# Issuing the first x load of a streaming kernel as two transfers, rows 0 to 15 and rows 16 to 127

## Chip, cores and metric

The kernel runs on one core of a Trainium2 chip. The metric is the device time in microseconds (us); lower is better. Runs of one kernel agree within about half a per cent here, with an occasional run 1% off. "Span" is the time from the first to the last instruction of the one profiled execution; the timed run is about 1.8 us longer (152.39 us for a span of 150.6 us).

## The reference

```python
B, S, D = 512, 32, 640          # bfloat16
def reference(x, fx, alpha):    # x, fx: [B, S, D]; alpha: [1]
    return x + alpha * fx
```

## The kernel before

The tensors are viewed as 128 rows of 81,920 bf16 elements, one row for each SBUF partition, and are worked through in five chunks of 16,384 columns. A chunk of x or fx is 128 rows of 32 KB, 4 MiB. All large transfers are issued by SyncE, in a fixed order. VectorE does one fused multiply-add for each chunk, in place in the x buffer, and the x buffer is then stored.

```python
xv = x.flatten_outer_dims().rearrange("(p n) d -> p (n d)", p=P)   # fxv, ov alike
xs = ctx.enter_context(tc.tile_pool(name="xs", bufs=4))
fs = ctx.enter_context(tc.tile_pool(name="fs", bufs=2))
ctx.enter_context(tc.manual_schedule())
# ... cut: alpha is put on all lanes by one tiny load, a matmul and a copy ...

def load_x(k):
    xt[k] = xs.tile([P, CHUNK], x.dtype, tag="x", name="x_t")
    nc.sync.dma_start(out=xt[k][:], in_=xv[:, bass.ts(k, CHUNK)])

def load_f(k):
    ft[k] = fs.tile([P, CHUNK], fx.dtype, tag="f", name="f_t")
    nc.sync.dma_start(out=ft[k][:], in_=fxv[:, bass.ts(k, CHUNK)])
# ... cut: compute(k, parts) is one scalar_tensor_tensor per part; store(k, j, parts) one DMA ...

load_x(0); load_f(0); load_x(1); load_f(1); load_x(2)
compute(0); load_f(2); store(0); load_x(3)
compute(1); load_f(3); store(1); load_x(4)
compute(2); load_f(4); store(2)
compute(3); store(3)
compute(4, 2); store(4, 0, 2); store(4, 1, 2)
```

## Time and profile before

| quantity | before |
|---|---|
| time, median of 4 runs | 152.93 us (152.51 to 153.17) |
| span of the profiled run | 150.6 us |
| bytes moved by DMA | 62.92 MB, 418 GB/s over the span |
| VectorE busy | 86.9 us, 58% |
| first compute starts | 22.84 us |

These lines are from the page of the kernel before: engine shares, the DMA rows of the 40 time slices (tenths of full, then GB/s), the DMA queues, the chain of waits that ended last, and the loads with their size and the time from issue to landing (the median, where a line holds several).

```profile
span 150.6 us, 85 instructions
PE 0.2 (0%) x1; PEld 0.1 (0%) x1; DVE 86.9 (58%) x8; POOL 0.2 (0%) x4
...
DMA  6999999999999999799999999999999999999994
GB/s 200 444 453 435 418 418 418 418 444 453 444 453 435 418 418 418 339 444 470 418 418 418 418 418 435 435 435 453 426 435 444 418 418 435 435 435 405 426 444 205
...
q1 hardware_dynamic: 2304, 62.92, 98.0%
...
DMA 56%; DVE 29%; DVEq 6%; issue 0%; SPq 0%
...
x_t<-in_x_dram SPq DMA_DIRECT2D x5, 4096.0 KB, 34.8
f_t<-in_fx_dram SPq DMA_DIRECT2D x5, 4096.0 KB, 32.1
```

The DMA engines are full from the second slice to the last but one. The chain of waits names VectorE for 29%, but while it computes, the queue behind it stays full, so I would not expect a faster VectorE to end the kernel sooner. The bound is the DMA stream.

The next lines are windows of the same run; the last two columns are the mean busy share of the 16 DMA engines and the GB/s they moved. A transfer's bytes are counted where their packet starts, so the GB/s of a short window swing around the true rate.

```profile
0.00:8.00 8.00, 0.16 (x1) 0.10 (x1) 0.32 (x2) 0.20 (x4) 1.00 0.85 328
8.00:16.00 8.00, 0.00 (x0) 0.00 (x0) 0.00 (x0) 0.00 (x0) 1.00 1.01 434
16.00:24.00 8.00, 0.00 (x0) 0.00 (x0) 1.16 (x1) 0.00 (x0) 1.00 0.97 418
```

And these are its computes in the timeline: start and duration in us, and in brackets how long VectorE had been idle and what ended the idle time.

```profile
22.84 17.28 DVE L69 SCALAR_TENSOR_TENSOR x_t<-f_t,a_f,x_t 128x16384 bf16<-128x16384 bf16 x1 [20.57 <-DMA f_t<-in_fx_dram]
42.25 17.28 DVE L69 SCALAR_TENSOR_TENSOR x_t<-f_t,a_f,x_t 128x16384 bf16<-128x16384 bf16 x1 [2.12 <-DMA f_t<-in_fx_dram]
62.24 17.28 DVE L69 SCALAR_TENSOR_TENSOR x_t<-f_t,a_f,x_t 128x16384 bf16<-128x16384 bf16 x1 [2.71 <-DMA f_t<-in_fx_dram]
91.71 17.29 DVE L69 SCALAR_TENSOR_TENSOR x_t<-f_t,a_f,x_t 128x16384 bf16<-128x16384 bf16 x1 [12.19 <-DMA f_t<-in_fx_dram]
120.91 17.42 DVE L69 SCALAR_TENSOR_TENSOR x_t<-f_t,a_f,x_t 128x8192 bf16<-128x8192 bf16 x2 [11.91 <-DMA f_t<-in_fx_dram]
```

The trace also holds a record of each packet (`prof` doesn't print them; they were read from the trace file). A packet here is one row of one transfer, 32 KB, moved by one of the 16 DMA engines; at 20, 30, 80 and 100 us of the span 16 of them are under way. The first row of each engine takes 1.6 to 2.4 us, and nearly all others take about 1.213 us, which is 27 GB/s for an engine. Each engine moves the equivalent of 120 such rows: 120 x 1.213 = 145.6 us of the 150.6 us span.

### The profile page before, as it was taken

To read this page: it belongs to the slowest core of one execution; us is meant where nothing else is said; L and a number is where in the kernel's file an instruction comes from. 1 tells how busy PE (TensorE), PEld (TensorE's weight loads), DVE (VectorE), ACT (ScalarE), POOL (GpSimd) and SP (SyncE) were. 2 spreads that over 40 slices of the span, in tenths; PEclk is the share of its full clock that TensorE was granted. 3 is DMA by queue.
4 is the path that set the end of the run, shared out by engine and by line. 5 is a ranking of instruction groups with operands and counts; after the bars stand their busy time and mean duration, and the time that the engine had idled before them with its cause. 6 is when DMAs were issued, how large, how long until landed. Compare 5 with 4: busy or idle time off the path is not lost.

```text
span 150.6 us, 85 instructions
## 1 busy us (share of the span) xinstructions
PE 0.2 (0%) x1; PEld 0.1 (0%) x1; DVE 86.9 (58%) x8; POOL 0.2 (0%) x4
## 2 busy tenths in 40 slices
PE   0000000000000000000000000000000000000000
PEld 0000000000000000000000000000000000000000
DVE  0000009999679998499991006999900089997000
POOL 0000000000000000000000000000000000000000
DMA  6999999999999999799999999999999999999994
GB/s 200 444 453 435 418 418 418 418 444 453 444 453 435 418 418 418 339 444 470 418 418 418 418 418 435 435 435 453 426 435 444 418 418 435 435 435 405 426 444 205
DMA packets 2306, 62.92 MB, mean 418 GB/s; under 512 B 258, under 2 KB 258, under 8 KB 258
## 3 DMA queue, kind: packets, MB, share of 16 engines
q1 hardware_dynamic: 2304, 62.92, 98.0%
q10 hardware_dynamic: 2, 0.00, 0.0%
HBM read 41.94 MB, written 20.97 MB: 418 GB/s over the span
## 4 chain that ended last, share of the span: by engine, by line
DMA 56%; DVE 29%; DVEq 6%; issue 0%; SPq 0%
DMA f_t<-in_fx_dram 56%; DVE x_t L69 29%; DVEq L131 6%; SPq L59 0%; DVEq L69 0%
## 5 line engine op out<-in xcount | busy, mean ns | idle before, releaser
L69 DVE SCALAR_TENSOR_TENSOR x_t<-f_t,a_f,x_t 128x16384 bf16<-128x16384 bf16 (+1 forms) x6 | 86.6, 14439 | 49.5 <-DMA f_t<-in_fx_dram 49.5
L26 DVE COPY a_f<-a_ps 128x1 f32<-128x1 f32 x1 | 0.2, 159 | 1.1 <-PE a_ps L24 1.1
L22 DVE MEMSET ones<- 1x128 bf16 x1 | 0.2, 165 | 0.8 <-PEq L120 0.8
L24 PE MATMUL a_ps<-a,ones 1*128 1x1 bf16 x1 | 0.2, 159 | 1.9 <-DMA a<-in_alpha_dram 1.9
L120 POOL MEMSET const-bfloat16-1.0<- 128x1 bf16 x1 | 0.1, 102 | 0.0
L120 POOL MEMSET const-uint8-127<- 128x1 uint8 x1 | 0.1, 102 | 0.0
L24 PEld LDWEIGHTS <-ones 1*128 1x128 bf16 x1 | 0.1, 100 | 1.0 <-DVE ones L22 1.0
L120 POOL MEMSET const-float32-0.0<- 128x1 f32 x1 | 0.1, 99 | 0.2 <-issue 0.2
L120 POOL MEMSET const-float32-1.0<- 128x1 f32 x1 | 0.1, 99 | 0.0
## 6 DMA issues: line engine op xcount, KB each, us to landing
x_t<-in_x_dram SPq DMA_DIRECT2D x5, 4096.0 KB, 34.8
f_t<-in_fx_dram SPq DMA_DIRECT2D x5, 4096.0 KB, 32.1
out_dram<-x_t SPq DMA_DIRECT2D x4, 4096.0 KB, 36.5
out_dram<-x_t SPq DMA_DIRECT2D x2, 2048.0 KB, 15.2
a<-in_alpha_dram ACTq DMA_DIRECT2D x1, 0.0 KB
```

What stands on the lines that cost most here:

```text
L22: nc.vector.memset(ones[:], 1.0)
L24: nc.tensor.matmul(a_ps[:], ones[:], a_1[:], start=True, stop=True)
L26: nc.vector.tensor_copy(out=a_f[:], in_=a_ps[:])
L69: nc.vector.scalar_tensor_tensor(out=xt[k][:, s], in0=ft[k][:, s], scalar=a_f[:], in1=xt[k][:, s], op0=ALU.mult, op1=ALU.add,)
L120: nc = _bacc.Bacc("TRN2", target_bir_lowering=False, num_devices=1)
L131: with _tile.TileContext(nc) as tc:
```

## The change

The likely intent is to get the DMA engines going sooner: a small transfer of 16 rows is put in front, and the other 112 rows follow at once. The bytes, the computes and the order of everything else stay as they are.

```diff
     def load_x(k):
         xt[k] = xs.tile([P, CHUNK], x.dtype, tag="x", name="x_t")
-        nc.sync.dma_start(out=xt[k][:], in_=xv[:, bass.ts(k, CHUNK)])
+        for a, b in [(0, 16), (16, P)] if k == 0 else [(0, P)]:
+            nc.sync.dma_start(out=xt[k][a:b, :], in_=xv[a:b, bass.ts(k, CHUNK)])
```

## The prediction

> **What bounds the kernel now.** DMA. The page's queue part gives 62.92 MB in a 150.6 us span and 98.0% of 16 engines' time; only the first and last slices are not full. DVE is busy 58%; on the chain of waits it appears (29%) only because it stands between transfers, while the queue stays full behind it. In the trace's packet records each of the 16 DMA engines moves 120 rows' worth of 32 KB at a median 1.213 us: 120 x 1.213 = 145.6 us. The rest is about 1.6 us before the first packet, 1.5 us of slower packets where stores begin, and 1.3 us of completion. Whatever slows all DMA engines anywhere is paid in full.
>
> **What the change does.** It removes no work and adds no bytes. It adds one issue on SyncE (0.38 to 0.57 us each in the timeline), hidden behind the first packets (1.6 to 2.4 us), and a second completion to wait for (tens of ns; DVE waits for f_t, not x_t). Possible gain: 16 rows may reach all engines sooner; before's first packets start over 0.42 us, so at most about 0.3 us.
>
> **The cost I expect** is how the rows meet SBUF. [...] Before's trace agrees only in that 128 rows run at 16 x 27 GB/s; it has no narrow load. Estimates with the trace's 1.213 us:
> - Rows 0 to 15 are one row per engine[...].
> - Rows 16 to 127 are 7 rows per engine. [...]
> - Together +3 to +8 us. [...]
>
> **On the critical path: all of it.** The queue never drains, so the delay moves f_t's first landing (22.7 us), every compute and the last store alike. Nothing later gives it back.
>
> **Prediction: 158.5 us**, 80% range 153.0 to 163.5. Faster by over 2%: 0.02; within 2%: 0.25; slower by over 2%: 0.73.
>
> **What would show each step.**
> - [...]
> - Collisions in the 112-row load: packets of about 2.4 us among the next 112, and engines out of step afterwards; then 1.213 us again.
> - Shift: the first DVE compute starts at 26 to 31 us instead of 22.8; later gaps are unchanged; the span grows by the same amount; DVE busy stays 86.9 us.
>
> **What would make it wrong.** If [...]engines have enough in flight to hide it, only tenths of a us remain: 152.9 to 153.5 us. [...]

The forecast's sum stands: +3 to +8 us, with 158.5 us (152.93 + 5.57) as the central value.

## The result and the profile after

| quantity | before | after |
|---|---|---|
| time, median of 4 runs | 152.93 us | 162.26 us (162.13 to 162.70) |
| span of the profiled run | 150.6 us | 160.4 us |
| bytes | 62.92 MB | 62.92 MB |
| VectorE busy | 86.9 us | 86.9 us |
| first compute starts | 22.84 us | 32.31 us |

The ratio is 1.0619, with a 95% interval of 1.0583 to 1.0654. A ratio is the mean time of one kernel's fast runs over that of the other's of the same rounds, so it is not quite the ratio of the medians. The changed kernel is slower by 6%.

The same lines of the page after the change:

```profile
span 160.4 us, 88 instructions
PE 0.2 (0%) x1; PEld 0.1 (0%) x1; DVE 86.9 (54%) x8; POOL 0.2 (0%) x4
...
DMA  9799999999999999999999999999999999999991
GB/s 131 139 261 286 253 351 441 449 417 425 449 433 400 457 441 400 441 466 400 433 449 425 425 449 417 408 449 441 417 417 474 392 417 466 417 425 425 400 445 53
...
q1 hardware_dynamic: 2320, 62.92, 97.1%
...
DMA 59%; DVE 27%; DVEq 5%; SPq 0%; issue 0%
...
f_t<-in_fx_dram SPq DMA_DIRECT2D x5, 4096.0 KB, 31.3
x_t<-in_x_dram SPq DMA_DIRECT2D x4, 4096.0 KB, 39.8
...
x_t<-in_x_dram SPq DMA_DIRECT2D x1, 3584.0 KB, 21.3
x_t<-in_x_dram SPq DMA_DIRECT2D x1, 512.0 KB, 7.2
```

The busy row of the DMA engines is as full as before, from the first slice on. Only the GB/s row below it shows the loss: five slices of about 4 us at 131 to 286 GB/s instead of some 430. The engines are busy, but with rows that take longer. The windows and the computes say the same:

```profile
0.00:8.00 8.00, 0.16 (x1) 0.10 (x1) 0.32 (x2) 0.20 (x4) 1.00 0.85 135
8.00:16.00 8.00, 0.00 (x0) 0.00 (x0) 0.00 (x0) 0.00 (x0) 1.00 1.01 270
16.00:24.00 8.00, 0.00 (x0) 0.00 (x0) 0.00 (x0) 0.00 (x0) 1.00 0.98 307
24.00:32.00 8.00, 0.00 (x0) 0.00 (x0) 0.00 (x0) 0.00 (x0) 1.00 1.03 442
```

```profile
32.31 17.29 DVE L70 SCALAR_TENSOR_TENSOR x_t<-f_t,a_f,x_t 128x16384 bf16<-128x16384 bf16 x1 [30.02 <-DMA f_t<-in_fx_dram]
51.71 17.28 DVE L70 SCALAR_TENSOR_TENSOR x_t<-f_t,a_f,x_t 128x16384 bf16<-128x16384 bf16 x1 [2.12 <-DMA f_t<-in_fx_dram]
71.13 17.29 DVE L70 SCALAR_TENSOR_TENSOR x_t<-f_t,a_f,x_t 128x16384 bf16<-128x16384 bf16 x1 [2.13 <-DMA f_t<-in_fx_dram]
100.43 17.28 DVE L70 SCALAR_TENSOR_TENSOR x_t<-f_t,a_f,x_t 128x16384 bf16<-128x16384 bf16 x1 [12.02 <-DMA f_t<-in_fx_dram]
130.55 17.41 DVE L70 SCALAR_TENSOR_TENSOR x_t<-f_t,a_f,x_t 128x8192 bf16<-128x8192 bf16 x2 [12.83 <-DMA f_t<-in_fx_dram]
```

The five computes start 9.47, 9.46, 8.89, 8.72 and 9.64 us later than before, and the span is 9.8 us longer. Nearly the whole loss thus arises before the first compute and stays. The packet records show where. Here are the first rows of each engine, sixteen records at a time in the order of their starts; before, the means are 1.93 us and then 1.21 to 1.23 us:

```
after: n-th row of the 16 engines, us: shortest / mean / longest
row 0 (the 16-row transfer)  2.40 / 3.73 / 4.31
row 1 (112-row transfer)     2.57 / 2.91 / 3.67
row 2                        2.18 / 2.25 / 2.29
row 3                        1.45 / 1.68 / 2.08
row 4                        1.68 / 1.85 / 2.20
row 5                        1.72 / 2.00 / 2.41
row 6                        2.02 / 2.15 / 2.22
row 7                        1.98 / 2.07 / 2.29
row 8 (fx load)              1.50 / 1.71 / 2.00
row 9                        1.21 / 1.23 / 1.27
```

### The profile page after: what moved, and what is told of

Read it like the earlier page. It is cut to its first block, busy times and chain, and to the rows that moved or that the text cites. A ratio compares the mean times of both kernels' runs of the same rounds, so it can differ in the third digit from the quotient of the medians.

```text
span 160.4 us, 88 instructions
## 1 busy us (share of the span) xinstructions
PE 0.2 (0%) x1; PEld 0.1 (0%) x1; DVE 86.9 (54%) x8; POOL 0.2 (0%) x4
## 2 busy tenths in 40 slices
DMA packets 2322, 62.92 MB, mean 392 GB/s; under 512 B 274, under 2 KB 274, under 8 KB 274
## 3 DMA queue, kind: packets, MB, share of 16 engines
q1 hardware_dynamic: 2320, 62.92, 97.1%
## 4 chain that ended last, share of the span: by engine, by line
DMA 59%; DVE 27%; DVEq 5%; SPq 0%; issue 0%
DMA f_t<-in_fx_dram 59%; DVE x_t L70 27%; DVEq L132 5%; SPq L60 0%; DVEq L70 0%
```

## The experiments

The main theory is that of the prediction: how long a row takes depends on which SBUF partitions the rows of its transfer hit. The texts call it the port theory. That engines meet and share something at some partitions, and the word "port" for it, are my guess: the traces show the time of each row, but no ports, and not which engine wrote which partition. "Consecutive" and "round robin" are two guesses of how the rows of a transfer are dealt to the engines, and no trace shows which it is. The rivals are:

- A: two transfers cost more than one, however they are cut (issue, completion, a small first transfer).
- B: a transfer of fewer than 128 rows is slow by its shape.
- C: it is the rows of HBM that matter.
- D, added later ("foreign port" in the texts): each engine is fast only to the partitions that it has in a 128-row load.

Runs called "extra" are the kernel before with one or more loads added at the very front of the queue, into a buffer that is loaded again with the proper data later; all of them give correct results. (Their diffs below show the added load alone.) In their traces, the start of the first compute, less 22.84 us, is what the load cost. The record does not name the chip of the trace of before, and the others come from three chips, but the median row takes 1.213 to 1.215 us in all of them. Each of these starts is read from one trace. Timed ratios are to runs of before on the same chip.

### The same split by columns

```diff
+        for a, b in [(0, 2048), (2048, CHUNK)] if k == 0 else [(0, CHUNK)]:
+            nc.sync.dma_start(out=xt[k][:, a:b], in_=xv[:, k * CHUNK + a : k * CHUNK + b])
```

> The first x load is again two transfers of one eighth and seven eighths of its bytes, but cut by columns (2048 and 14336 of 16384), so that both have 128 rows. Port theory (the loss comes from which SBUF partitions the rows of a transfer hit): nothing is lost, 152.5 to 153.8 us, first compute at 22.4 to 23.2 us. Rival A (two transfers, one more issue, one more completion or a small first transfer cost the time, however they are cut): about 162 us as after the change, first compute at about 32 us.

Measured: 153.00 us against 152.84 us for before, ratio 1.0026 (0.9966 to 1.0085): no difference. The loads in the page of this run, and its first compute:

```profile
x_t<-in_x_dram SPq DMA_DIRECT2D x1, 3584.0 KB, 11.5
x_t<-in_x_dram SPq DMA_DIRECT2D x1, 512.0 KB, 3.3
```

```profile
22.56 17.29 DVE L70 SCALAR_TENSOR_TENSOR x_t<-f_t,a_f,x_t 128x16384 bf16<-128x16384 bf16 x1 [20.27 <-DMA f_t<-in_fx_dram]
```

The same two sizes, the same number of issues and completions, and no loss: rival A falls. The first 512 KB land 3.3 us after issue when cut by columns and 7.2 us when they are rows 0 to 15, a difference of 3.9 us. The first compute starts 0.28 us sooner than before, about the gain that the change may have been after. That is one trace against one; the time does not show a gain, and by the last compute the two kernels are level (120.94 and 120.91 us).

### Sixty-four rows, two places

```diff
+    nc.sync.dma_start(out=xt[3][0:64, :], in_=xv[0:64, bass.ts(3, CHUNK)])    # one run
+    nc.sync.dma_start(out=xt[3][32:96, :], in_=xv[0:64, bass.ts(3, CHUNK)])   # the other
```

> The kernel before with one extra load put first on the queue: 64 rows of 32 KB into partitions 0 to 63 of a buffer that is not needed until later. Its bytes alone are 4 rows per DMA engine, 4 x 1.213 = 4.85 us. Port theory with consecutive rows per engine: [...]162.4 to 163 us. [...] Rival B (a transfer of fewer than 128 rows is slow by its shape alone, whatever its partitions): the same time as the next run. No effect of either: 157.8 us.

> The same extra load of the same 64 rows of HBM, but into partitions 32 to 95. Port theory with 4 consecutive rows per engine: [...]157.5 to 158.3 us, 4 to 5.2 us less than the run at partition 0. [...] Rival B (shape) and rival C (the rows in HBM): the same time as the run at partition 0.

Measured: 162.97 us at partition 0 (ratio 1.0668, interval 1.0611 to 1.0725) and 158.15 us at partition 32 (1.0365, 1.0312 to 1.0417), with 152.84 us for before. The extra load's line in the page, first at partition 0, then at partition 32:

```profile
x_t<-in_x_dram SPq DMA_DIRECT2D x1, 2048.0 KB, 13.5
```

```profile
x_t<-in_x_dram SPq DMA_DIRECT2D x1, 2048.0 KB, 7.7
```

Shape, bytes and HBM rows are the same; only the SBUF partitions differ, and 4.8 us come and go with them. Rivals B and C fall. In the packet records the rows at partition 0 take 2.57 us after the first, and those at partition 32 take 1.21 to 1.26 us on average.

### Eight transfers of sixteen rows

```diff
+        for a, b in [(16 * i, 16 * i + 16) for i in range(8)] if k == 0 else [(0, P)]:
+            nc.sync.dma_start(out=xt[k][a:b, :], in_=xv[a:b, bass.ts(k, CHUNK)])
```

> The first x load cut into eight transfers of 16 rows. Each gives one row to each engine[...]. Port theory, engines that cannot run ahead: [...]about 177 to 182 us. Port theory, engines that run ahead by most of a row: about 163 to 167 us. If the 112 rows of the changed kernel are dealt round robin, they are the same as seven such transfers, and this run equals the changed kernel, 162 us; if they are consecutive, it is slower than that. Rival A (a cost for each transfer added): 153 + 7 x 9.3 = 218 us. No dependence on rows: 153 to 156 us.

Measured: 177.76 us, ratio 1.1620 (1.1572 to 1.1668). The GB/s row of its page:

```profile
GB/s 119 119 119 119 119 119 119 119 238 402 431 469 372 469 439 394 476 402 431 469 387 454 431 402 476 402 424 439 402 469 424 417 431 417 439 446 409 413 431 227
```

The time is in the range expected for engines that cannot run ahead (177 to 182 us), and much less than the 218 us of a cost for each transfer. It is also far slower than the changed kernel (162.26 us), so the 112 rows there do not cost what seven transfers of 16 rows do. Rows 1 to 7 of each engine take 4.46 us on average in the packet records, 3.7 times the 1.213 us of a row in a 128-row load; the timeline agrees, with SyncE's next four issues 4.45 to 4.47 us apart (8.14, 12.59, 17.05 and 21.52 us).

### The two halves of the change by themselves

```diff
+    nc.sync.dma_start(out=xt[3][0:16, :], in_=xv[0:16, bass.ts(3, CHUNK)])          # 16 rows
+    nc.sync.dma_start(out=xt[3][0:128:8, :], in_=xv[0:16, bass.ts(3, CHUNK)])       # 16 rows, spread
+    nc.sync.dma_start(out=xt[3][0:128, 0:2048],                                     # same bytes, 128 rows
+                      in_=xv[0:128, 3 * CHUNK : 3 * CHUNK + 2048])
+    nc.sync.dma_start(out=xt[3][16:128, :], in_=xv[16:128, bass.ts(3, CHUNK)])      # 112 rows
```

(One of these lines in each run.)

> The kernel before with an extra load of 16 rows of 32 KB into partitions 0 to 15 of the idle buffer, first on the queue: the first half of the change measured by itself. Its bytes are one row per engine, 1.213 us. Port theory: [...]157.3 to 158.2 us. No port effect for so short a load: 154.1 us.

> The same 16 rows of HBM and the same 16 descriptors, but into every eighth partition (0, 8, ... 120)[...]. Port theory: [...]154.9 to 155.8 us, about 2.4 us less than with partitions 0 to 15. Rival B (a load of 16 rows is slow because of its shape): the same as with partitions 0 to 15.

> The same 512 KB as 128 rows of 4 KB, into all partitions. Port theory: only the bytes, 1.2 us, so 153.8 to 154.5 us. It shows what 512 KB more cost[...].

> The kernel before with an extra load of 112 rows into partitions 16 to 127 of the idle buffer: the second half of the change by itself. Its bytes are 7 rows per engine, 8.5 us, so 161.4 us without collisions. Port theory with consecutive rows and fair sharing, no running ahead: [...]166.2 us. If the halves add up, [...]the run takes about 167 us. [...]

| extra load | time (before: 153.34 us) | ratio, interval | landing after issue | first compute later by | its bytes alone | loss (later by, less bytes) |
|---|---|---|---|---|---|---|
| 16 rows, partitions 0 to 15 | 156.15 us | 1.0190 (1.0142 to 1.0237) | 6.9 us | 4.20 us | 1.21 us | 2.99 us |
| 16 rows, every 8th partition | 155.01 us | 1.0125 (1.0078 to 1.0172) | 5.4 us | 2.61 us | 1.21 us | 1.40 us |
| 128 rows of 4 KB | 153.92 us | 1.0053 (1.0010 to 1.0095) | 3.9 us | 1.32 us | 1.21 us | 0.11 us |
| 112 rows, partitions 16 to 127 | 167.74 us | 1.0941 (1.0883 to 1.0999) | 17.4 us | 14.81 us | 8.49 us | 6.32 us |

The order is as expected: the same 512 KB cost least on all 128 partitions (first compute later by 1.32 us), more on every 8th partition (2.61 us) and most on partitions 0 to 15 (4.20 us). From one to the next the times differ by about 1.1 us, and the intervals of neighbours overlap; the order stands more clearly in the landings and first computes. The size for 16 rows was missed: 156.15 us is below the 157.3 to 158.2 us expected, and 1.14 us above the run with every 8th partition where about 2.4 us were expected. Why the short load costs less than expected is not shown. The 112 rows cost more than the 166.2 us of the estimate with fair sharing, and about the 167 us expected if the halves add up. The first computes of the runs with 16 rows on partitions 0 to 15 and with 112 rows, from which the losses are taken:

```profile
27.04 17.29 DVE L70 SCALAR_TENSOR_TENSOR x_t<-f_t,a_f,x_t 128x16384 bf16<-128x16384 bf16 x1 [24.74 <-DMA f_t<-in_fx_dram]
37.65 17.28 DVE L70 SCALAR_TENSOR_TENSOR x_t<-f_t,a_f,x_t 128x16384 bf16<-128x16384 bf16 x1 [35.36 <-DMA f_t<-in_fx_dram]
```

At the first compute the halves do add up: 2.99 + 6.32 = 9.31 us, against 9.47 us in the changed kernel.

In the packet records of the 112-row run the seven rows take 2.05 us on average, and after the first row no engine has a row below 1.65 us. That was unexpected: by my estimate, which no trace shows, only some of the 16 engines would meet at any step. The last four runs ask why all of them were slow.

### Sixty-four rows, two more places

```diff
+    nc.sync.dma_start(out=xt[3][36:100, :], in_=xv[0:64, bass.ts(3, CHUNK)])   # one run
+    nc.sync.dma_start(out=xt[3][48:112, :], in_=xv[0:64, bass.ts(3, CHUNK)])   # the other
```

"Independent" stands for engines that slow down without slowing the others, "coupled" for all being slowed together. How many engines would meet at each place was my estimate.

> The extra load of 64 rows again, now into partitions 36 to 99. [...] It asks why the 112 rows slowed all 16 engines alike (rows of 1.65 to 2.3 us each)[...]. Theory independent: most rows of the extra load take 1.21 us, 2 of 16 take 2.4 or more. Theory coupled[...]: all 16 engines' rows are longer, about 2 us. [...]

> The same into partitions 48 to 111[...]. Independent: half of the rows 1.21 us, half 2.4 us or more. Coupled: all rows longer[...], at most 2.57 us. [...]

Measured, with the two runs above for comparison (before: 152.93 us for the two new ones, two runs of each). Row 0 is an engine's first row, which is slower for nearly all of them (before: 1.93 us on average, then 1.21 to 1.23 us). The packet records do not name the engine; I followed an engine by matching the start of each row to the end of the one before.

```
64 rows at  rows 1 to 3 of the extra load, us        lands after  first compute  time, us
partition                                            issue, us    later by, us
32          nearly all 1.21 to 1.33, one 1.55        7.7           5.14          158.15
36          14 of 16 engines 1.21 to 1.39, 2: 2.47+  14.8         11.92          163.40
48          all 16 engines 2.49 to 2.54              12.5          9.94          162.04
0           all 16 engines 2.52 to 2.58              13.5         10.70          162.97
```

Here are the page lines of the extra load, at partition 36 and then at 48:

```profile
x_t<-in_x_dram SPq DMA_DIRECT2D x1, 2048.0 KB, 14.8
```

```profile
x_t<-in_x_dram SPq DMA_DIRECT2D x1, 2048.0 KB, 12.5
```

At partition 36, 14 engines run at full speed beside two slow ones, as expected for "independent". Yet this run is as slow as the one at partition 0 (ratios 1.0673 and 1.0668), and its first compute is the latest of the four. The trace tells why: it holds 16 records of the landing of each transfer, as many as there are engines. Fourteen parts of the extra load land by 8.71 us of the run, and two only at 15.25 and 15.51 us. Of the next load 13 parts land by 19.65 us and three at 23.07, 24.50 and 24.91 us. The rows of these late engines take up to 4.03 us; why is not shown. In that time the rows of the other engines take 1.52 us and not 1.21 us, so even here the others are slowed in the end. The computes wait for the last part: the first fx chunk of the kernel before lands from 22.11 to 22.72 us and the first compute starts at 22.84 us, after the change 30.80 to 32.18 us and 32.31 us. So three late engines can hold up the first compute and everything after it. At partition 48 all 16 parts land between 12.44 and 13.24 us and all 16 engines are slow, as expected for "coupled", where "independent" had half of the rows at 1.21 us. So neither "independent" nor "coupled" holds throughout.

### Four loads of eight rows, two places

```diff
+    for j in range(4):                                       # one run: START = 0, other: START = 64
+        nc.sync.dma_start(out=xt[0][START + j : START + j + 29 : 4, :],
+                          in_=xv[8 * j : 8 * j + 8, bass.ts(3, CHUNK)])
```

> Control of the next run: four extra loads of 8 rows each (rows every fourth partition from 0, 1, 2, 3 on), into x0's own buffer, so that the x0 load waits for them and nothing runs beside them. Eight engines carry 4 rows each[...]. All theories: first rows 1.5 to 2.3 us, then 1.21 to 1.25 us each.

> The same with partitions from 64, 65, 66, 67 on[...]. Foreign port theory: rows longer than 1.25 us after the first, the loads land later by 3 us or more. Coupled or independent port sharing: the same as the run from partition 0, within 0.3 us.

Measured: 161.67 and 161.83 us (before 152.93 us), first computes at 30.88 and 31.32 us. The eight engines' second and fourth rows take 1.21 to 1.27 us in both runs, but six and three of the eight third rows are longer (up to 1.68 and 2.25 us), in the control too, where I had expected none. The difference of 0.44 us is a little over the 0.3 us that I allowed, but nowhere near the 3 us expected for rival D, so D finds no support. (That the engines at partition 64 write partitions other than their own of a 128-row load was my estimate; no trace shows it.) Both runs are slow against before because x0 waits until these loads have landed: it is issued at 8.85 and 9.42 us, and not at 0.73 us.

## Why the prediction was right

- **The bound** was read rightly. Nothing that delays all DMA engines at the start is given back in substance: 9.47 us at the first compute, 9.8 us in the span, about 9.3 us in the time. A small part does move: before waits 2.71 us for the third fx chunk, the changed kernel 2.13 us, and the last computes lose it again. The first compute, at 32.31 us, came later than the 26 to 31 us that I named.
- **The mechanism** was right as far as it was tested: the time follows the SBUF partitions of a transfer (64 rows at partition 0 or 32: 4.8 us apart) and not the number of transfers (the split by columns: no loss). That engines share ports there was my guess and is not shown.
- **The 16 rows**: the landing is 3.9 us later than that of the same bytes cut by columns (7.2 and 3.3 us). At the first compute, 2.99 us of it remain when a 128-row load follows. The first packets took 2.4 to 4.3 us, and the first 6 us ran at 142 GB/s (before: 262 GB/s). The record of a row closes before the row has landed: the 16 rows' records end at 4.16 to 6.41 us, but the landings come at 6.25 to 7.90 us, some 1.5 to 2 us later, against 0.4 us for the first load of the kernel before. So the wait is spread over two rows. In the run with the extra 16 rows alone the means of the first two rows add up to 6.11 us, against 3.16 us before.
- **The 112 rows** are the larger part of the loss: 6.32 us of the 9.31 us of both halves. The central 158.5 us left only 5.57 us for both halves together. In the run with the 112 rows alone all 16 engines take about 2.05 us per row. My total of +3 to +8 us was short of the 9.3 us measured, and the central 158.5 us was 3.8 us low, though 162.26 us lies in the 80% range of 153.0 to 163.5 us. That range was wider than the sum of the steps, so the hit in time is in part luck.
- **The possible gain** of up to 0.3 us is not shown: one trace of the split by columns has the first compute 0.28 us sooner, but the time has no gain.
- **Left open:** what slows the rows, and what couples the engines. At partition 36 two slow engines left the other 14 alone in their own load (1.21 to 1.39 us), and in the next load, while the late engines' rows took up to 4.03 us, the others' took 1.52 us; at partition 48 (2.49 to 2.54 us) and with the 112 rows (2.05 us on average) all 16 were slow. No run here isolates the cause.

## What to carry to other kernels

For a kernel bound by DMA, this case speaks for cutting a transfer along the free dimension and not along the partitions. It was tested on one load at the start of one kernel: by columns the split cost nothing (ratio 1.0026), by rows 9.3 us, 6% of the whole kernel. The even split by rows was not run, but one half of it was, as an extra load: 64 rows on partitions 0 to 63 took 2.57 us a row and not 1.21 us. In the 128-row loads of the kernel before, 97% of the 32 KB rows were within 5% of 1.213 us; with a part of the partitions that pace held for 64 rows in one place (32 to 95) and not in the three others tried, and at partition 36 late engines ran into the next transfer. To see it in a profile, compare the GB/s row with the busy row: in the first slices here the engines are full at a third of their rate (131 and 139 GB/s instead of some 430), moving rows that take longer. The duration of single rows shows it too (1.213 us in a 128-row load, 2.57 us for 64 rows at partition 0, 4.46 us for 16 rows at a time), but does not tell the cause: at partition 48, where one of the theories had half of the rows at 1.21 us, all engines took about 2.5 us, as at partition 0.
